# Loading 32 partitions of one expert's weights as four 8-partition DMAs, each followed by a tiny read

## The chip, the cores and the metric

The kernel runs on one core of one Trainium2 chip. The metric is device time in microseconds (us) of one execution. Most executions of one kernel agree within 0.3 to 0.5%. A time is "faster" or "slower" only when the 95% interval of the ratio leaves the band of 2% around one.

## The reference

The program is an attention layer followed by a soft mixture of experts. Cut to what matters:

```python
# q, k, v: (8 batches, 8 heads, 576, 64), fp32
scores = scale * q @ k^T          # heads 0-3: window of 32; heads 4-7: window of 128, every 4th
attn   = softmax(scores) @ v
x      = attn, heads side by side # (4608, 512)

logits = x @ phi                  # (4608, 32): 8 experts x 4 slots
slot_input = softmax(logits, over rows)^T @ x          # (32, 512)
for e in range(8):                                     # w1[e]: (512, 1024), w2[e]: (1024, 512), fp32
    slot_out[e] = relu(slot_input[e] @ w1[e]) @ w2[e]
out = softmax(logits, over slots) @ slot_out           # (4608, 512)
```

What matters for this change: the weights `w1` and `w2` are 2 MB per expert each and are read once, the output can't begin before the last expert's `w2` has landed, and nothing can be loaded usefully after that.

## The kernel before

All DMAs are issued by POOL on one queue. They convert fp32 in HBM to fp16 in SBUF while they copy. The weights of the experts are requested far ahead, between the attention batches. The loads of `w2`:

```python
def load_w2(e, half=None):
    if half is None:                       # one DMA: all 128 partitions, 1024 KB written
        nc.gpsimd.dma_start(
            out=w2t[e].rearrange("p (h l) n -> p h (l n)", h=2),
            in_=moe_w2[e].rearrange("(h p l) n -> p h (l n)", h=2, l=4),
        )
        return
    src = moe_w2[e].rearrange("(h p l) n -> h p l n", h=2, l=4)
    c0 = NH * half
    for h in range(2):                     # two DMAs: half of the columns, 256 KB written each
        nc.gpsimd.dma_start(
            out=w2t[e][:, 4 * h : 4 * h + 4, c0 : c0 + NH], in_=src[h][:, :, c0 : c0 + NH]
        )
```

The order in which they are requested; `weights(b, g)` is called twice in each batch b:

```python
HALVED = (6, 7)
ORDER = (0, 1, 4, 2, 3, 5) + HALVED

def weights(b, g):
    if b < B - 2:
        load_w1(*next_w1.pop(0))
    elif b == B - 2:
        if g == 0:
            ...                            # what is left of w1
            load_w2(0)
            load_w2(1)
        else:
            slab_weights(4, "vs0", V_SLAB) # expert 4 takes over a buffer of attention
            load_w2(4)
    elif g == 0:
        ...
        for e in (2, 3):
            w2t[e] = pool.tile([128, 8, DMODEL], FP16, name=f"w2_{e}", tag=f"w2_{e}")
            load_w2(e)
    else:
        slab_weights(5, "vs1", V_SLAB)
        load_w2(5)
        slab_weights(6, "qk0", QK_SLAB)
        slab_weights(7, "v0", V_SLAB)
        for half in range(2):
            for e in HALVED:
                load_w2(e, half)           # eight halved DMAs, the last loads of the program
```

The matmuls of `slot_out` use `w2` in `ORDER`, first for the left half of the output's columns, then for the right half. When the left halves of experts 6 and 7 have landed, the left half of the output is written while the right halves still load:

```python
slot_out(0, ORDER[:6])
slot_out(1, ORDER[:6])
slot_out(0, HALVED)
at = {5: 0}
for pair in range(NSPLIT // 2):
    combine(0, pair)                       # output rows, left columns: matmul, scale, DMA out
    if pair in at:
        slot_out(1, (HALVED[at[pair]],))
slot_out(1, HALVED[1:])
for pair in range(NSPLIT // 2, NFIN // 2):
    combine_full(pair)                     # further rows, all columns
```

The softmax here doesn't subtract the row's maximum and nothing guards it: scores larger than these inputs give would overflow.

Of the kernel before, what the change touches and what calls it, by code (L numbers as in the profile page):

```python
# [10 lines left out]
FP16 = mybir.dt.float16  # L11
# [38 lines left out]
def kernel(  # L50
# [10 lines left out]
    nc = tc.nc  # L61

    consts = ctx.enter_context(tc.tile_pool(name="consts", bufs=1))
    masks = consts.tile([128, W1 + NLEFT], FP16, name="masks")
    halves = consts.tile([128, 1], FP32, name="halves")
    bias = (
        masks[:, None, 0:WQ].broadcast_to([128, 3, WQ]),
        masks[:, 0 : W1 + NLEFT],
# [18 lines left out]
    w2t = {e: w2a_pool.tile([128, 8, DMODEL], FP16, name=f"w2_{e}", tag=f"w2_{e}") for e in range(2)}  # L87
# [12 lines left out]
    for i in range(NV):  # L100
        slab = fix.tile([128, V_SLAB], FP16, name=f"v{i}", tag=f"v{i}")
        n = NT * 4 * VW
# [5 lines left out]
    def slab_weights(e, tag, n):  # L108
        t = fix.tile([128, n], FP16, name=f"w2_{e}", tag=tag)
        w2t[e] = t[:, 0 : 8 * DMODEL].rearrange("p (c n) -> p c n", c=8)  # L110
# [99 lines left out]
    def load_w1(e, i):  # L210
        nc.gpsimd.dma_start(  # L211
            out=w1t[e][:, 2 * i : 2 * i + 2, :].rearrange("p l f -> p (l f)"),
            in_=moe_w1[e, 256 * i : 256 * i + 256].rearrange("(p l) f -> p (l f)", l=2),
        )

    def load_w2(e, half=None):
        if half is None:
            nc.gpsimd.dma_start(
                out=w2t[e].rearrange("p (h l) n -> p h (l n)", h=2),
                in_=moe_w2[e].rearrange("(h p l) n -> p h (l n)", h=2, l=4),  # L220
            )
            return
        src = moe_w2[e].rearrange("(h p l) n -> h p l n", h=2, l=4)
        c0 = NH * half
        for h in range(2):
            nc.gpsimd.dma_start(  # L226
                out=w2t[e][:, 4 * h : 4 * h + 4, c0 : c0 + NH], in_=src[h][:, :, c0 : c0 + NH]
            )
# [8 lines left out]
    def qk_dil(ti, b, part):  # L237
        src = raw[(ti, b)][:, 1, :].bitcast(U32)
        t = (qTd if ti == 0 else kTd)[b % 2]
        dst = t.rearrange("p s t -> p (s t)").bitcast(U32)  # L240
        base, n, step, j0 = ((0, 5, 292, 0), (2 * SUB, 4, -283, 2))[part]
        o = bass.AP(dst.tensor, dst.offset + base, [dst.ap[0], (SUB, 2), (1, n), (9, 16), (step, 2)])
        i = bass.AP(src.tensor, src.offset + 32 * j0, [src.ap[0], (32, 2), (128, n), (1, 32)])
        nc.vector.transpose(out=o, in_=i)  # L244
# [217 lines left out]
    def prologue():  # L462
# [56 lines left out]
            qk_dil(0, 0, part)  # L519
        qk_dil(1, 0, 0)  # L520

    HALVED = (6, 7)
    ORDER = (0, 1, 4, 2, 3, 5) + HALVED
    late_pools = []
# [6 lines that stand above are left out]
                while next_w1:  # L531
# [4 lines that stand above are left out]
                slab_weights(4, "vs0", V_SLAB)  # L536
                load_w2(4)
        elif g == 0:
            raw_pool.release()
            pool = tc.alloc_tile_pool(name="w2b", bufs=1, side="right")  # L540
            late_pools.append(pool)
            for e in (2, 3):
                w2t[e] = pool.tile([128, 8, DMODEL], FP16, name=f"w2_{e}", tag=f"w2_{e}")
                load_w2(e)
        else:
            slab_weights(5, "vs1", V_SLAB)
            load_w2(5)
            slab_weights(6, "qk0", QK_SLAB)
            slab_weights(7, "v0", V_SLAB)
            for half in range(2):  # L550
                for e in HALVED:
                    load_w2(e, half)

    def slot0(b):
        att, b1, b2, b3 = b < B, b - 1 >= 0 and b <= B, 2 <= b < B + 2, b + 1 < B
        if att:
            qk_dil(1, b, 1)
            emit_scores(b, 0)
            if b + 2 < B:
                load_qk(0, b + 2)  # L560
                load_qk(1, b + 2)
            weights(b, 0)
# [29 lines left out]
    def slot1(b):  # L592
        att, b1, b3 = b < B, 1 <= b <= B, b + 1 < B
        if b3:
            qk_plain(0, b + 1)
        if att:
            emit_scores(b, 1)
            if b == 0:
                order_v_plain(b)
            spread_v(b)  # L600
            if b + 2 < B:
                load_v(b + 2)
            weights(b, 1)
            emit_av(b, "p", 0)
            emit_norm(b, "p", 0)
        if b1:
            back_xT_dil(b - 1, 0)
        if b3:
            qk_plain(1, b + 1)
        if b1:  # L610
            back_xT_dil(b - 1, 1)
# [41 lines left out]
    for g in range(4):  # L653
# [8 lines left out]
        out=diag,  # L662
# [7 lines left out]
    for fc in range(2):  # L670
        for g in range(2):
            for dc in range(4):
                for j in range(4):
                    e = 4 * g + j
# [32 lines left out]
    def slot_out(half, experts):  # L707
        for e in experts:
            for c in range(8):
                g, j, a = e // 4, e % 4, c % 4  # L710
                nc.tensor.matmul(
                    so[half][32 * a : 32 * a + 32, :],
                    hTm[2 * g + c // 4][:, c % 4, 32 * j : 32 * j + 32],
                    w2t[e][:, c, NH * half : NH * half + NH],
                    start=(e == ORDER[0] and c < 4),
                    stop=(e == ORDER[-1] and c >= 4),
                )
        if experts[-1] == ORDER[-1]:
            nc.scalar.copy(out=so_sb[:, NH * half : NH * half + NH], in_=so[half])
# [75 lines left out]
    with tc.manual_schedule(engines=None):  # L795
# [5 lines that stand above are left out]
            combine(0, pair)  # L801
# [4 lines that stand above are left out]
# [39 lines left out]
```

## Time and profile before

| | before |
|---|---|
| median of three runs (lowest to highest) | 183.85 us (183.4 to 183.96) |
| span in the profile, mean granted clock of TensorE | 182.0 us, 0.902 |
| last landing of expert 5's `w2` | 145.26 us |
| last `w2` DMA: first engine lands, last engine lands | 152.23 us, 155.98 us |
| last landing of an output DMA | 179.27 us |

The landing times in the last three rows come from the completion events in the trace: it holds sixteen of them for every DMA (1,472 for 92 DMAs), which I take for one report from each of the sixteen DMA engines. "Last landing" is the sixteenth report; the "spread" of a DMA is the time from its first report to its last.

These lines are from the page of the kernel before. In the first two each entry is one of 40 equal slices of the span: the busy tenths of the sixteen DMA engines, and what they moved. Then come two DMA queues (packets, megabytes, share of the engines' time) and the shares of the chain of work that ended last.

```profile
DMA  4999999999999999999999999999999999999992
GB/s 61 194 195 210 202 211 212 204 212 214 201 213 214 201 212 216 200 212 212 205 210 215 202 215 213 214 213 214 216 214 216 195 196 181 355 404 404 409 409 59
...
q0 software_dynamic: 29248, 40.41, 117.6%
q8 instruction: 19, 0.31, 0.6%
...
DMA 40%; PE 37%; ACT 6%; DVE 5%; POOL 4%; issue 3%; POOLq 0%
```

The DMA engines are busy in nearly every slice, at about 195 to 216 GB/s while fp32 is read and fp16 is written, and at about 404 to 409 GB/s while results are written. So the kernel is bound by the DMA engines from the first load to the last store.

This is POOL's timeline of the kernel before: start, duration, engine, line and operation, output and input, count; in brackets, how long POOL had been idle just before and what ended the wait. L218 is a whole `w2` DMA, here the one of expert 5, and L226 a halved one.

```profile
116.29 0.72 POOL L218 DMA_DIRECT2D w<-in_moe_w_dram  x1
117.00 1.49 POOL L226 DMA_DIRECT2D w<-in_moe_w_dram  x2
120.25 0.74 POOL L226 DMA_DIRECT2D w<-in_moe_w_dram  x1 [1.76 <-ACT p L292]
124.95 0.74 POOL L226 DMA_DIRECT2D w<-in_moe_w_dram  x1 [3.96 <-DMA w<-in_moe_w_dram]
129.92 0.74 POOL L226 DMA_DIRECT2D w<-in_moe_w_dram  x1 [4.22 <-DMA w<-in_moe_w_dram]
...
145.54 0.74 POOL L226 DMA_DIRECT2D w<-in_moe_w_dram  x1 [4.21 <-DMA w<-in_moe_w_dram]
```

Expert 5 and the first halved DMA are requested at 116 to 117 us and land at 145.3 and 146.6 us, so the queue holds almost 30 us of work. The waits from 124.95 us on show how deep it may get. Each issue waits for the landing of the DMA issued eight before it: the issue at 124.95 comes 0.28 us after the landing, at 124.67, of the DMA issued at 102.18. The trace agrees: the completions are counted on eight semaphores in turn. I call these the eight places. There is always something in the queue, which the windows of the kernel before show near the end of the loads (start and end, width, busy time and count of PE, PE's weight loads, DVE, ACT and POOL, then granted clock, DMA share, GB/s; the share can exceed one, as that of q0 does on the page):

```profile
146.00:148.00 2.00, 1.21 (x48) 1.01 (x37) 0.00 (x0) 0.00 (x0) 0.28 (x1) 1.00 1.45 195
148.00:150.00 2.00, 0.50 (x8) 0.12 (x8) 0.00 (x0) 0.00 (x0) 0.00 (x0) 0.93 1.45 196
150.00:152.00 2.00, 0.88 (x7) 0.56 (x7) 0.00 (x0) 0.44 (x2) 0.00 (x0) 0.50 1.45 196
```

The DMA rate doesn't move from 195 GB/s, while PE idles between halved DMAs. The sixteen engines don't keep step. These are the sixteen completion times of two DMAs of the kernel before, sorted, counted from the first:

```
expert 5, landing 141.54 to 145.26:  0.0 0.1 0.3 0.4 0.5 0.5 1.1 1.2 2.1 2.2 2.2 2.2 2.7 2.8 3.2 3.7
last w2,  landing 152.23 to 155.98:  0.0 0.1 0.3 0.5 0.5 0.5 1.1 1.2 2.1 2.2 2.2 2.7 2.8 3.3 3.3 3.8
```

Eight engines are 0 to 1.2 us behind the first, the other eight 2.1 to 3.8 us. The kernel's end hangs on the slowest one. That is the imbalance which the change wants to use.

### The profile page before, as it was taken

Reading aid. Unit: us, or ns where it says so; the run is one execution under the profiler, and the core shown is the slowest. Engines: PE = TensorE matmul, PEld = TensorE weight load, DVE = VectorE, ACT = ScalarE, POOL = GpSimd, SP = SyncE. Lnnn points to the kernel's source line nnn. Section 1 sums busy time; section 2 is a strip of 40 time slices with the busy share of each in tenths; the row PEclk is TensorE's granted clock in tenths of the full one; section 3 lists DMA queues with packets and bytes.
Section 4 is the critical chain, followed back from the end, with each engine's and each line's share of the span. In section 5 each row is a group of like instructions: output and inputs, shape, how many; then the busy total and the mean of one; then the engine's idle time right before and its main releaser. Section 6 shows DMA issues by size and latency. Waiting matters only on the chain.

```text
span 182.0 us, 5571 instructions
## 1 busy us (share of the span) xinstructions
PE 143.0 (79%) x2464; PEld 85.3 (47%) x2464; DVE 107.1 (59%) x232; ACT 90.4 (50%) x162; POOL 80.8 (44%) x118
## 2 busy tenths in 40 slices
PE   0467987999999999999999999999879447885000
PEld 0234545656646746746746746746443334331000
DVE  4688785865884984984984984445041104597000
ACT  2044355847557657657657657655101105696000
POOL 7954563634624434432631625621111014999700
PEclk9999998798799999999999999999756995799755
DMA  4999999999999999999999999999999999999992
GB/s 61 194 195 210 202 211 212 204 212 214 201 213 214 201 212 216 200 212 212 205 210 215 202 215 213 214 213 214 216 214 216 195 196 181 355 404 404 409 409 59
DMA packets 29271, 40.75 MB, mean 224 GB/s; under 512 B 1600, under 2 KB 19008, under 8 KB 29248
## 3 DMA queue, kind: packets, MB, share of 16 engines
q0 software_dynamic: 29248, 40.41, 117.6%
q8 instruction: 19, 0.31, 0.6%
q14 instruction: 4, 0.03, 0.0%
HBM read 61.93 MB, written 9.44 MB: 392 GB/s over the span
## 4 chain that ended last, share of the span: by engine, by line
DMA 40%; PE 37%; ACT 6%; DVE 5%; POOL 4%; issue 3%; POOLq 0%
DMA w<-in_moe_w_dram 26%; DMA raw<-in_k_dram 10%; PE lg L407 6%; PE o_p L338 5%; PE sa L281 4%; ACT p L292 4%; PE sa L270 4%; DMA out_dram<-ot 3%; PE sb L270 3%; PE f L745 2%; PE vb L162 2%; PE va L162 2%; PE rd L388 2%; PE u L451 2%; POOL out_dram L791 1%
## 5 line engine op out<-in xcount | busy, mean ns | idle before, releaser
L292 ACT ACTIVATE p<-sa 128x960 f16<-128x960 f32 (+2 forms) x24 | 21.4, 891 | 31.2 <-PE sb L281 30.6
L338 PEld LDWEIGHTS <-p 128*128 128x128 f16 (+2 forms) x544 | 19.8, 99 | 12.8 <-issue 8.6
L244 DVE STREAM_TRANSPOSE qk<-raw 128x320 uint32<-128x320 uint32 (+1 forms) x32 | 21.6, 679 | 0.3
L292 ACT ACTIVATE p<-sb 128x960 f16<-128x960 f32 (+2 forms) x24 | 21.2, 884 | 0.0
L235 DVE STREAM_TRANSPOSE qk<-raw 128x576 uint32<-128x576 uint32 x16 | 19.8, 1249 | 1.5 <-DMA raw<-in_k_dram 1.1
L211 POOL DMA_DIRECT2D w<-in_moe_w_dram x16 | 8.8, 553 | 26.3 <-DMA vs<-in_v_dram 12.7
L270 PE MATMUL sa<-masks,ident 128*128 128x480 f16 (+2 forms) x48 | 14.6, 390 | 7.3 <-POOL masks L488 6.2
L407 PE MATMUL lg<-xTd,phi 128*128 128x288 f16 x32 | 18.2, 657 | 0.0
L270 PEld LDWEIGHTS <-ident 128*128 128x128 f16 x96 | 9.1, 106 | 17.9 <-issue 7.0
L281 PEld LDWEIGHTS <-qk 32*128 32x128 f16 x832 | 12.3, 98 | 11.1 <-issue 8.9
L338 PE MATMUL o_p<-v,p 128*128 128x65 f16 (+1 forms) x288 | 16.8, 203 | 0.8 <-ACT v L171 0.7
L281 PE MATMUL sa<-qk 32*128 32x160 f16 (+4 forms) x416 | 16.2, 215 | 0.8 <-DVE qk L235 0.7
L226 POOL DMA_DIRECT2D w<-in_moe_w_dram x8 | 5.9, 744 | 23.3 <-DMA w<-in_moe_w_dram 21.6
L281 PE MATMUL sb<-qk 32*128 32x160 f16 (+4 forms) x416 | 16.3, 215 | 0.0
L360 DVE TENSOR_TENSOR xp<-o_p,rc_p 128x448 f16<-128x448 f32 (+1 forms) x24 | 14.4, 602 | 0.8
L360 DVE TENSOR_TENSOR xd<-o_d,rc_d 128x448 f16<-128x448 f32 (+1 forms) x24 | 14.4, 602 | 0.8
L270 PE MATMUL sb<-masks,ident 128*128 128x480 f16 (+2 forms) x48 | 14.4, 386 | 0.2 <-ACT p L292 0.2
L208 POOL COPY v<-v 32x1024 f16<-32x1024 f16 x8 | 8.3, 1036 | 11.3 <-DVE v L201 9.9
L162 PE MATMUL va<-vs,orders 32*128 32x256 f16 (+1 forms) x96 | 12.1, 289 | 1.0 <-ACT p L292 1.0
L411 ACT ACTIVATE ET<-lg 128x288 f16<-128x288 f32 x16 | 6.6, 411 | 11.8 <-PE lg L407 11.7
L381 ACT COPY xTp<-rp 128x576 f16<-128x576 f16 x16 | 10.4, 647 | 1.8 <-PE rp L376 1.8
L767 POOL DMA_DIRECT2D out_dram<-ot x15 | 10.8, 719 | 0.0
(102 smaller groups left out, 266.4 us busy)
## 6 DMA issues: line engine op xcount, KB each, us to landing
w<-in_moe_w_dram POOLq DMA_DIRECT2D x16, 512.0 KB, 17.0
w<-in_moe_w_dram POOLq DMA_DIRECT2D x6, 1024.0 KB, 25.3
out_dram<-of POOLq DMA_DIRECT2D x10, 512.0 KB, 6.2
vs<-in_v_dram POOLq DMA_DIRECT2D x8, 512.0 KB, 17.0
raw<-in_q_dram POOLq DMA_DIRECT2D x7, 576.0 KB, 18.2
raw<-in_k_dram POOLq DMA_DIRECT2D x7, 576.0 KB, 18.5
out_dram<-ot POOLq DMA_DIRECT2D x15, 256.0 KB, 4.9
w<-in_moe_w_dram POOLq DMA_DIRECT2D x8, 256.0 KB, 23.8
```

Of the source, the lines that this page charges most:

```text
L162: nc.tensor.matmul(o.rearrange("p (h d) -> p h d", h=4), l, st[:, 0:4, D * r : D * r + D], start=(r == 0), stop=(r == DIL - 1), skip_group ...
L211: nc.gpsimd.dma_start(out=w1t[e][:, 2 * i : 2 * i + 2, :].rearrange("p l f -> p (l f)"), in_=moe_w1[e, 256 * i : 256 * i + 256].rearrange( ...
L235: nc.vector.transpose(out=dst, in_=src)
L244: nc.vector.transpose(out=o, in_=i)
L270: nc.tensor.matmul(sps[h // 2][:, h % 2, 0:n], ident, bias[g], start=True, stop=False, skip_group_check=True,)
L281: nc.tensor.matmul(sps[h // 2][:, h % 2, c0 : c0 + w], kt_[32 * h : 32 * h + 32, k0 : k0 + 128, tt], qt_[32 * h : 32 * h + 32, q0 : q0 + w ...
L292: nc.scalar.activation(out=pt, in_=sps[ab][:, :, 0:n], func=AF.Exp, scale=SCALE)
L338: nc.tensor.matmul(o[p0 : p0 + np_, n, :], l, rr, start=(k == 0), stop=(k == len(jobs) - 1), skip_group_check=True,)
L360: nc.vector.tensor_tensor(out=x.rearrange("p t (h d) -> p (t h) d", h=4)[0:nq, u0:u1, :], in0=o[0:nq, 0:n, 0:D], in1=rc[0:nq, 0:n, None].b ...
L381: nc.scalar.copy(out=xTp_t[b][:, c, :], in_=rg)
L407: nc.tensor.matmul(lp, phi4[:, kc].rearrange("p c s -> p (c s)"), rhs, start=(kc == 0), stop=(kc == 3))
L767: nc.gpsimd.dma_start(out=out[r0 : r0 + 256, NH * half : NH * half + NH].rearrange("(k p) n -> p k n", k=2), in_=ot,)
```

## The change

The intent: an 8-partition DMA should be carried by eight of the sixteen DMA engines only. The last 32 partitions of expert 2 are taken out of its large DMA and requested as four DMAs over 8 partitions each (rows 96+j, 100+j, ...). After each of them stands a tiny read of 8 rows of 32 bytes, which should use the other eight engines, so that the next 8-partition DMA returns to the first eight. The data of 32 partitions would then lie on the eight engines that have time left, and the slow eight would have less to carry. The whole diff:

```diff
@@ constants
+    turn = consts.tile([128, 8], FP16, name="turn")
@@ load_w2
-    def load_w2(e, half=None):
+    def load_w2(e, half=None, rows=slice(0, 128)):
         if half is None:
             nc.gpsimd.dma_start(
-                out=w2t[e].rearrange("p (h l) n -> p h (l n)", h=2),
-                in_=moe_w2[e].rearrange("(h p l) n -> p h (l n)", h=2, l=4),
+                out=w2t[e].rearrange("p (h l) n -> p h (l n)", h=2)[rows],
+                in_=moe_w2[e].rearrange("(h p l) n -> p h (l n)", h=2, l=4)[rows],
             )
             return
@@ before weights
+    def load_w2_eight(e, j):
+        load_w2(e, rows=slice(96 + j, 128, 4))
+        nc.gpsimd.dma_start(out=turn[0:8, :], in_=moe_w2[e, 0:8, 0:8])
+
@@ weights, last batch
                 w2t[e] = pool.tile([128, 8, DMODEL], FP16, name=f"w2_{e}", tag=f"w2_{e}")
-                load_w2(e)
+                load_w2(e, rows=slice(0, 96 if e == 2 else 128))
         else:
             slab_weights(5, "vs1", V_SLAB)
+            load_w2_eight(2, 0)
             load_w2(5)
+            for j in range(1, 4):
+                load_w2_eight(2, j)
             slab_weights(6, "qk0", QK_SLAB)
```

Below, d0 to d3 are the four 8-partition DMAs of data and r0 to r3 the four tiny reads. All four reads write the same 8 by 8 elements of `turn`, which nothing uses.

## The prediction

> **What bounds the kernel now.** The page's DMA row is 9 in nearly every slice (200-216 GB/s while fp32 is read and fp16 written, 404-409 GB/s while results are written): DMA-bound from about 5 to 179 us. The sixteen completion events of each DMA in the trace show that engines do not keep step: the last w2 transfer lands between 152.2 us (first engine) and 156.0 us (last). Eight engines lag 0-1.2 us, eight 2.2-3.8 us. Eighteen instruction packets of 16 KB (0.9 us each, durations repeating with period eight) run between 18 and 140 us, and the lags grow in steps of about 1.1 us, so eight engines seem to carry all instruction fetches. (Trainium skill, "Runtime: NRT & Kernel Launch", Instruction fetch mechanics: 16 KiB blocks on the sequencer's own queue; the trace agrees: queue 8, 16,384 B.) The slowest engine is never idle: last weights 155.98 + 9.44 MB of output at 405 GB/s (23.3 us) = 179.3 us; the last landing is 179.27.
>
> **Intent and gain.** The Trainium skill ("DMA: Bandwidth & Descriptors", How many engines) says an 8-partition DMA goes to 8 consecutive engines from a cursor; no trace here shows it yet. The tiny read on the other eight returns the cursor, so all 32 partitions land on the same eight engines: 10 partitions of expert 2 there, 6 on the others. A 128-partition w2 DMA (8 per engine) takes 4.9 us, so a partition is 0.61 us: -1.22 us on one half, +1.22 us on the other. If the fetching half is relieved, the best case is -1.2 us (182.6).
>
> **Cost.** POOL's timeline shows each DMA waiting for the landing of the one eight issues earlier (issue at 124.95 waits for that of 102.18, landed 124.67). Eight small DMAs now fill these places. And all four tiny reads write the same tile, so I expect each to wait until the previous one has landed (write after write). Read 0 lands behind w2(3), near 139.1 us (140.3 - 1.2). Read 1 then goes behind w2(5), landing near 144.1. Read 2 goes into an almost empty queue, landing near 145.9 (0.5 us issue, 0.7 to first packet, 0.6 to land, estimated from the first DMA and the output DMA at 152.7). Read 3 goes then, and the first halved w2 DMA only at about 146.4, first packet 147.6; in before these eight were queued from 117 us on. They take 10.7 us (145.26 to 155.98): end near 158.9 instead of 156.0. Half 0 is complete near 153.5 instead of 150.6, and the outputs shift as much, all on the critical path: +2.9 us. If the strided row slices (97,101.. against 96,100..) also count as overlapping, another +0.9 us. PE, ACT, DVE have slack.
>
> **Prediction.** 186.9 us, 80% range 183.5 to 188.4. Faster by over 2%: 0.02; within: 0.65; slower: 0.33.
>
> **What would show it.** POOL's timeline: read 1 waiting to about 139, read 2 to about 144, eight halved w2 issues back to back (0.74 us) from 146-147 us. DMA row: a hole near 144-147.5 us. Completion spread of the last w2 DMA about 1 us instead of 3.8; of w2(5) nearer 2.5 than 3.7 if the fetching half was relieved, about 5 if loaded. PE: the so matmuls (L711) wait for w2 to 153-154 us. Output DMAs as in before, shifted.
>
> **What would make it wrong.** If the reads do not wait for each other, only the eight places bind: halves from about 139.7 us, no hole, 182.5-185, the sign set by which half the cursor picks. If rows overlap, 187.7. If small DMAs land later than 1.7 us in an emptying queue, more.

## The result, and the profile after

| | before | after |
|---|---|---|
| median of four runs (lowest to highest) | 183.91 us (183.4 to 184.42) | 191.68 us (190.96 to 192.04) |
| span in the profile, granted clock | 182.0 us, 0.902 | 190.0 us, 0.874 |
| first halved DMA issued | 117.00 | 147.94 |
| expert 5's `w2`, last landing | 145.26 | 144.47 |
| last `w2` DMA, first and last landing | 152.23, 155.98 | 161.10, 163.35 |
| last landing of an output DMA | 179.27 | 186.65 |

The kernel after is slower: the ratio is 1.0418, with a 95% interval of 1.0376 to 1.046. A ratio is the mean time of one kernel's fast runs over the mean of the other's fast runs of the same rounds, so it isn't quite the ratio of the medians quoted. The time lies above the predicted range of 183.5 to 188.4 us.

The page of the kernel after, the same lines as above:

```profile
DMA  4999999999999999999999999999991699999990
GB/s 67 195 202 205 211 211 215 201 210 212 208 208 212 208 213 204 209 213 207 208 212 205 213 214 215 214 214 216 211 185 20 91 177 212 375 358 405 412 405 8
...
q0 software_dynamic: 29504, 40.41, 113.1%
q8 instruction: 19, 0.31, 0.6%
...
PE 45%; DMA 24%; ACT 8%; POOL 7%; DVE 6%; issue 4%; POOLq 0%
...
L525 POOL DMA_DIRECT2D turn<-in_moe_w_dram x4 | 2.1, 530 | 24.8 <-DMA turn<-in_moe_w_dram 24.8
```

The same 40.41 MB are moved, in 256 more packets. The thirty-first slice (142.5 to 147.25 us) holds a hole: 20 GB/s where the kernel before has 216 in its thirty-first slice. The group line of the four reads says why: POOL was busy for 2.1 us with them and stood for 24.8 us in front of them, waiting for a DMA into `turn`.

POOL's timeline of the kernel after, with the columns as before. L219 is a whole or 8-partition DMA of `w2`, L525 a tiny read, L227 a halved DMA.

```profile
116.00 0.58 POOL L219 DMA_DIRECT2D w<-in_moe_w_dram  x1
116.58 0.54 POOL L525 DMA_DIRECT2D turn<-in_moe_w_dram  x1
117.10 0.75 POOL L219 DMA_DIRECT2D w<-in_moe_w_dram  x1
119.81 0.57 POOL L219 DMA_DIRECT2D w<-in_moe_w_dram  x1 [1.95 <-DMA w<-in_moe_w_dram]
139.90 0.53 POOL L525 DMA_DIRECT2D turn<-in_moe_w_dram  x1 [19.52 <-DMA turn<-in_moe_w_dram]
140.41 0.58 POOL L219 DMA_DIRECT2D w<-in_moe_w_dram  x1
145.25 0.53 POOL L525 DMA_DIRECT2D turn<-in_moe_w_dram  x1 [4.26 <-DMA turn<-in_moe_w_dram]
145.77 0.59 POOL L219 DMA_DIRECT2D w<-in_moe_w_dram  x1
147.42 0.53 POOL L525 DMA_DIRECT2D turn<-in_moe_w_dram  x1 [1.06 <-DMA turn<-in_moe_w_dram]
147.94 5.93 POOL L227 DMA_DIRECT2D w<-in_moe_w_dram  x8
```

From top to bottom: d0, r0, expert 5, d1, r1, d2, r2, d3, r3, and the eight halved DMAs. r1 waits 19.5 us until r0 has landed (139.61 us, behind expert 3 in the queue), r2 until r1 has landed (144.97, behind expert 5), and r3 until r2 has landed (146.87). While r1 waits, nothing behind it is issued. The queue drains, expert 5 lands at 144.47 us, and the halved DMAs, which were queued since 117 us in the kernel before, go out only from 147.94 us. The windows of the kernel after:

```profile
144.00:146.00 2.00, 0.00 (x0) 0.00 (x0) 0.00 (x0) 0.00 (x0) 0.75 (x2) 0.91 0.04 6
146.00:148.00 2.00, 0.00 (x0) 0.00 (x0) 0.00 (x0) 0.00 (x0) 0.94 (x3) 0.50 0.21 29
148.00:150.00 2.00, 1.16 (x24) 1.04 (x28) 0.00 (x0) 0.00 (x0) 2.00 (x3) 0.50 0.26 28
150.00:152.00 2.00, 2.00 (x45) 1.72 (x41) 0.00 (x0) 0.00 (x0) 2.00 (x4) 0.50 1.25 165
152.00:154.00 2.00, 0.85 (x23) 0.61 (x13) 0.00 (x0) 0.00 (x0) 1.86 (x3) 0.88 1.31 163
154.00:156.00 2.00, 0.45 (x8) 0.21 (x8) 0.00 (x0) 0.00 (x0) 0.00 (x0) 0.97 1.39 183
156.00:158.00 2.00, 0.65 (x8) 0.21 (x4) 0.00 (x0) 0.37 (x1) 0.00 (x0) 0.50 1.46 197
```

For six us, next to nothing moves. Then the rate is 163 to 165 GB/s for four us, 183 for two more, and reaches the 195 to 197 GB/s of the kernel before only after 156 us. The granted clock is 0.5 in some of these windows, but PE isn't what the time hangs on: after 152.8 us it waits again for halved DMAs, as in the kernel before. Next is the chain that ended last in the kernel before, in order of time (start, duration, what it was):

```profile
102.18 22.49 DMA w<-in_moe_w_dram
124.67 0.28 issue
124.95 25.66 DMA w<-in_moe_w_dram
```

And the same of the kernel after:

```profile
116.58 23.03 DMA turn<-in_moe_w_dram
139.90 5.07 DMA turn<-in_moe_w_dram
145.25 1.61 DMA turn<-in_moe_w_dram
...
153.12 10.23 DMA w<-in_moe_w_dram
```

The chain before is two weight DMAs linked by a freed place. After, it is three tiny reads, one behind the other, and then the last halved DMA. Notice that the share of DMA in this chain fell, from 40% to 24%, and yet the DMA engines still decide the end. A share of the chain doesn't say which resource has no slack.

From the last landing of `w2` on, everything is only shifted. The outputs end 23.29 us after it before and 23.30 us after it after. So the 7.37 us by which the last `w2` comes later (155.98 to 163.35) is the whole shift of the last output (7.38 us). The span grew by 8.0 us and the median by 7.8; the remaining 0.6 us of the span lies behind the last output's landing and wasn't looked into.

### The profile page after: what moved, and what is told of

Its sections match the earlier page's. It is cut to its first block, busy times and chain, and to the rows that moved or that the text cites. A ratio compares the mean times of both kernels' runs of the same rounds, so it can differ in the third digit from the quotient of the medians.

```text
span 190.0 us, 5584 instructions
## 1 busy us (share of the span) xinstructions
PE 144.8 (76%) x2464; PEld 86.9 (46%) x2464; DVE 107.2 (56%) x232; ACT 90.4 (48%) x162; POOL 85.0 (45%) x126
## 3 DMA queue, kind: packets, MB, share of 16 engines
q0 software_dynamic: 29504, 40.41, 113.1%
## 4 chain that ended last, share of the span: by engine, by line
PE 45%; DMA 24%; ACT 8%; POOL 7%; DVE 6%; issue 4%; POOLq 0%
DMA turn<-in_moe_w_dram 16%; PE lg L408 8%; ACT p L293 7%; PE o_p L339 7%; PE sa L282 6%; DMA w<-in_moe_w_dram 5%; PE sa L271 5%; PE sb L271 4%; DMA out_dram<-ot 3%; PE u L452 3%; PE vb L163 3%; PE va L163 3%; PE rd L389 2%; POOL w L227 2%; DVE of L792 2%
## 5 line engine op out<-in xcount | busy, mean ns | idle before, releaser
L212 POOL DMA_DIRECT2D w<-in_moe_w_dram x16 | 8.8, 553 | 26.9 <-DMA vs<-in_v_dram 12.5
L719 PE MATMUL so<-w,hTm 128*32 128x256 f16 x128 | 7.4, 371 | 11.2 <-DMA turn<-in_moe_w_dram 6.0
L361 DVE TENSOR_TENSOR xd<-o_d,rc_d 128x448 f16<-128x448 f32 (+1 forms) x24 | 14.5, 602 | 0.8
L361 DVE TENSOR_TENSOR xp<-o_p,rc_p 128x448 f16<-128x448 f32 (+1 forms) x24 | 14.5, 602 | 0.8
L525 POOL DMA_DIRECT2D turn<-in_moe_w_dram x4 | 2.1, 530 | 24.8 <-DMA turn<-in_moe_w_dram 24.8
```

Source lines behind the costliest of these rows:

```text
L212: nc.gpsimd.dma_start(out=w1t[e][:, 2 * i : 2 * i + 2, :].rearrange("p l f -> p (l f)"), in_=moe_w1[e, 256 * i : 256 * i + 256].rearrange( ...
L361: nc.vector.tensor_tensor(out=x.rearrange("p t (h d) -> p (t h) d", h=4)[0:nq, u0:u1, :], in0=o[0:nq, 0:n, 0:D], in1=rc[0:nq, 0:n, None].b ...
```

## The experiments

Three theories to begin with. A: the cost is the chain of reads through one tile (each read waits for the one before), and with it the empty queue. B: the cost is the eight places, which eight small DMAs take up. C: the 8-partition DMAs of data are slow themselves, or load the wrong eight engines. The diffs are cut to the lines that matter. The first four kernels ran on one chip, beside eleven runs of the kernel before with a median of 183.87 us.

### own_columns: the reads get columns of their own

```diff
-    turn = consts.tile([128, 8], FP16, name="turn")
+    turn = consts.tile([128, 32], FP16, name="turn")
-        nc.gpsimd.dma_start(out=turn[0:8, :], in_=moe_w2[e, 0:8, 0:8])
+        nc.gpsimd.dma_start(out=turn[0:8, 8 * j : 8 * j + 8], in_=moe_w2[e, 0:8, 0:8])
```

> The changed kernel, but each tiny read writes its own eight columns of the turn tile, so no read has to wait for another; same number, order and size of DMAs. Chain theory (the loss is the reads waiting for each other): the first halved w2 DMA is issued near 140 us instead of 147.9, no hole in the DMA row, time 183 to 185 us. Rival 1 (eight more DMAs in eight places are the loss): the second halved DMA waits for w2 expert 5 (near 144.5 us) and the time stays above 188 us. Rival 2 (uneven engines are the loss): time stays above 188 us and the last w2 DMA has a spread over 5 us.

Measured: 186.89 us, ratio 1.0178 (1.015 to 1.0207). The chain of waits between the reads is gone, and that gives back 4.8 of the 7.8 us. But the time is still 3 us above the kernel before (by the 2% rule this is "unclear", as the interval reaches over 1.02), which is outside of what I expected. POOL's timeline of own_columns shows the rest:

```profile
139.48 0.53 POOL L525 DMA_DIRECT2D turn<-in_moe_w_dram  x1
140.00 0.80 POOL L227 DMA_DIRECT2D w<-in_moe_w_dram  x1
144.65 5.13 POOL L227 DMA_DIRECT2D w<-in_moe_w_dram  x7 [3.86 <-DMA w<-in_moe_w_dram]
```

The second halved DMA waits until 144.65 us, for expert 5, which landed at 144.37. It was issued eight before, and all the places between are taken by d1 to d3, r1 to r3 and one halved DMA. When it goes, little but one halved DMA is in the queue. This is theory B at work, and the windows of own_columns show its smaller hole, 60 GB/s and then 134 to 147 where the kernel before has 195:

```profile
144.00:146.00 2.00, 1.33 (x44) 1.07 (x48) 0.00 (x0) 0.33 (x1) 1.35 (x2) 1.00 0.44 60
146.00:148.00 2.00, 1.63 (x60) 1.43 (x53) 0.00 (x0) 0.00 (x0) 2.00 (x4) 1.00 1.16 147
148.00:150.00 2.00, 0.29 (x4) 0.10 (x4) 0.00 (x0) 0.00 (x0) 1.79 (x3) 1.00 1.14 141
```

So A and B aren't exclusive: with the chain removed, the places bind and cost about 3 us.

### other_half: the read stands before its data

Own columns as above, and the two lines of `load_w2_eight` exchanged. If a tiny read passes the turn to the other eight engines, this puts the data on the other eight.

> As own_columns, but each tiny read goes before its data DMA, so that the cursor, if there is one, puts the data on the other eight engines. Cursor-and-skew theory: this run and own_columns differ by up to 2.4 us, the spread of the last w2 DMA being about 2.5 us where the data went to the eight engines without instruction fetches and 5 to 6 us where it went to the fetching ones. If the cursor does not matter, or each half has as many fetching engines, the two agree within 0.5 us.

Measured: 186.95 us, ratio 1.0173 (1.0147 to 1.0199), 0.06 us from own_columns. So exchanging read and data makes no difference in time here. That it puts the data on the other half isn't shown; the pairs further down speak against it.

### no_reads: the four data DMAs without the reads

```diff
         load_w2(e, rows=slice(96 + j, 128, 4))
-        nc.gpsimd.dma_start(out=turn[0:8, :], in_=moe_w2[e, 0:8, 0:8])
```

> The four data DMAs over 8 partitions without the tiny reads; with a cursor the data alternates between the halves and both carry 8 partitions. Chain theory: no chain, only four more DMAs than before: within 0.5 us of before (183.5 to 184.5). Rival (small DMAs themselves are dear): over 186 us.

Measured: 184.24 us, ratio 1.002 (0.9996 to 1.0043). Against theory C: to request 32 partitions as four DMAs costs 0.4 us, by the interval at most 0.8. With four small DMAs instead of eight, halved DMAs are queued from 129.94 us on.

### reads_alone: the four reads without the split data

```diff
     def load_w2_eight(e, j):
-        load_w2(e, rows=slice(96 + j, 128, 4))
         nc.gpsimd.dma_start(out=turn[0:8, :], in_=moe_w2[e, 0:8, 0:8])
@@ expert 2 is loaded whole
-                load_w2(e, rows=slice(0, 96 if e == 2 else 128))
+                load_w2(e, rows=slice(0, 128))
```

> Expert 2 is loaded whole as before; the four tiny reads into one tile stand where the change has them. Chain theory: the reads alone bring nearly the whole loss: first halved w2 DMA issued near 148 us, hole in the DMA row from about 145 to 149 us, time 190.5 to 192.5 us. Rival 2 (uneven engines): within 1 us of before.

Measured: 191.31 us, ratio 1.0433 (1.0394 to 1.0472). Four reads of 256 bytes, which carry nothing, bring the whole loss. They add only four DMAs, as no_reads does, so theory B isn't needed for it. With own_columns, where the chain goes and 4.8 us come back, this shows that A is the cause. The halved DMAs are issued from 148.43 us on, and the last `w2` lands at 162.96.

### What the pairs do to the sixteen engines

The intended gain never came, in any kernel. In the next two kernels the four pairs move to a quiet place: expert 0 instead of expert 2, one pair in each of batches 2 to 5, so that no wait and no hole can hide an effect. In spread_pairs each read stands behind its data, in spread_turned before it.

```diff
             load_w1(*next_w1.pop(0))
+            if g == 0 and 2 <= b < 6:
+                load_w2_eight(0, b - 2)
@@ expert 0
-                load_w2(0)
+                load_w2(0, rows=slice(0, 96))
```

> The four data-and-read pairs taken off expert 2 and given to expert 0, whose tile is free from the start: one pair in each of four batches of the attention stage, each read into its own columns. Same bytes, same 32 partitions on eight engines, but at most two small DMAs in the eight places at a time and none near the end. If the data lands on the eight engines without instruction fetches, as own_columns suggests (the seven or eight engines that lag least finish its small data DMA about 0.5 us after the DMA before, most others 0.2 us), the last w2 DMA spreads 2.5 us instead of 3.8 and the time is 182.5 to 183.2 us, 0.7 to 1.2 under before. If it lands on the fetching ones: spread 5 us, 185 us. If placement does not matter: within 0.3 us of before.

> As spread_pairs with the read ahead of its data DMA. If a cursor chooses the eight engines, this goes the other way from spread_pairs (about 185 us, spread about 5 us, or the reverse). If the engines follow from the partitions written, both agree within 0.4 us.

Measured: 184.41 us (ratio 1.0027, 1.0008 to 1.0046) and 184.21 us (1.0007, 0.9987 to 1.0026), beside 183.96 us. The completion times of the last `w2` spread over 3.5 and 4.0 us, against 3.8 in the kernel before. A concentration of 32 partitions on eight engines should have moved this by about 1.2 us one way in one kernel and the other way in the other. It did neither (spread_pairs is 0.45 us above the kernel before by the medians, a little more than the 0.3 us forecast for "placement does not matter"); this is a miss of the intended mechanism itself.

pairs_8 doubles the dose: eight pairs, over experts 0 and 1, one at every turn of batches 2 to 5. pairs_512 makes each read larger, 512 columns of 8 rows, in case 32 bytes a row are too few to count (the reads use three column blocks in rotation).

```diff
+            if 2 <= b < 6:
+                load_w2_eight(g, b - 2)
...
-        nc.gpsimd.dma_start(out=turn[0:8, :], in_=moe_w2[e, 0:8, 0:8])
+        c = 8 * (4 * e + j)                                                         # pairs_8
+        nc.gpsimd.dma_start(out=turn[0:8, c : c + 8], in_=moe_w2[e, 0:8, 0:8])
or
+        c = 512 * ((2 * j + e) % 3)                                                 # pairs_512
+        nc.gpsimd.dma_start(out=turn[0:8, c : c + 512], in_=moe_w2[e, 0:8, 0:512])
```

> As spread_pairs, but for experts 0 and 1: eight data-and-read pairs, one in each slot of four batches. If the tiny read brought the choice of engines back, eight engines would now carry 64 partitions alone, 4.9 us of work more than the other eight: the spread of the last w2 DMA would be 2.5 to 3 us in the opposite sense or over 6 us, and the time at least 1 us away from before. If the tiny read does not turn it, data alternates, every engine carries the same, the spread stays 3.4 to 4.2 us and the time within 1 us of before.

> As pairs_8, but each read takes 512 columns (2048 B a row, 1024 B written) in place of 8 columns (32 B). If only a larger read turns the choice of engines, the spread of the last w2 DMA becomes over 6 us (187 us or more) or the sense of the lag turns over. If reads of neither size turn it, this agrees with pairs_8 within 0.7 us.

Measured: 184.99 us (1.0043, 1.0 to 1.0086) and 184.62 us (1.0036, 1.0002 to 1.007), beside 183.93 us. The completion times of pairs_8, sorted and counted from the first, cut to a few of the sixteen:

```
before the pair:          0.0 0.1 0.1 0.1 0.3 0.4 0.7 0.8 ... 2.5
after one data DMA:       0.0 0.5 0.6 0.7 0.8 1.0 1.1     ... 3.0
after the next data DMA:  0.0 0.0 0.1 0.3 0.5 0.7 0.7 0.9 ... 2.5
```

One 8-partition DMA moves a part of the engines out of line, and the next one brings them back. The first of the sixteen reports shows it eight times over: from the DMA before it to the data DMA it moves by 0.28, 0.63, 0.26, 0.63, 0.22, 0.64, 0.17 and 0.63 us, and 0.61 us is the work of one partition. So consecutive data DMAs go to different halves and level each other out, although a read stands between them. (pairs_8 lies just outside of what was forecast for this: 1.06 us above the kernel before and a spread of 4.31 us, where within 1 us and 3.4 to 4.2 were expected; pairs_512 has 3.25.)

The last pair of kernels asks this more directly and has no reads at all. Each group of 8 partitions is loaded as two DMAs of unequal size, columns 0 to 1535 and 1536 to 2047. If same-shaped DMAs alternate between two halves of the engines, the large ones all fall on one half, and exchanging the two moves them to the other.

```diff
     def load_w2_eight(e, j):
-        load_w2(e, rows=slice(96 + j, 128, 4))
-        nc.gpsimd.dma_start(out=turn[0:8, :], in_=moe_w2[e, 0:8, 0:8])
+        for cols in (slice(0, 1536), slice(1536, 2048)):     # exchanged in unequal_small_first
+            load_w2(e, rows=slice(96 + j, 128, 4), cols=cols)
```

> As pairs_8, but instead of data and a wasted read, each group of 8 partitions comes as two useful DMAs of the same form, first three quarters of the columns, then one quarter. pairs_8 and pairs_512 showed the lags going out of line after one data DMA and back after the next, so consecutive data DMAs go to different halves whatever the read between. If the halves alternate for DMAs of one form, eight engines now get 48 partitions' worth and the other eight 16, 2.45 us of work apart: spread of the last w2 DMA about 2 to 2.7 us and a time of 182.5 to 183.3 us if the lagging half is relieved, over 5.5 us and 185 us if it is loaded. If the choice is not by alternation: spread 3.2 to 4.3 us and within 1 us of before.

> As unequal_big_first with the quarter ahead of the three quarters. If the halves alternate, this is the mirror image: where that one gains, this one loses by about as much, 2 us or more apart. If not, the two agree within 0.5 us.

Measured: 184.81 us (1.0057, 1.0036 to 1.0079) and 186.28 us (1.0138, 1.0115 to 1.0161), beside 183.87 us. The order of the two is worth 1.47 us in time, and 1.35 us in the last landing of `w2` (156.12 and 157.47 us). That lies between the two forecasts (2 us or more apart, or within 0.5), and neither kernel got faster. It fits the alternation that pairs_8 shows: load can be placed on one half by size. But even in the better order the slowest engines aren't relieved. The sorted times of its last `w2` are these:

```
0.0 0.3 2.0 2.1 2.2 2.2 2.3 2.3 2.5 2.6 2.9 3.0 3.1 3.3 4.2 4.3
```

Six engines that had slack were filled, two were not, and the two worst are at 4.2 and 4.3 us, where the worst of the kernel before is at 3.8. My reading is that the eight engines of a half aren't the eight that lag, so that no order of halves can help them; this is argued from these lines, not shown. Why the tiny read doesn't take part in the alternation stays open. None of these versions beats the kernel before.

### What an empty queue costs

The prediction knew the chain of reads and the hole, and still was 4.8 us too low (it gave 0.65 to a time within 2% of the kernel before and 0.33 to a slower one). What was open: after the hole the eight halved DMAs took longer than I had allowed. whole_after loads experts 6 and 7 of the kernel after as two large DMAs instead of eight halved ones, whole_before does it to the kernel before. If small DMAs or strided 512-byte runs make the restart slow, it should vanish.

```diff
-            for half in range(2):
-                for e in HALVED:
-                    load_w2(e, half)
+            for e in HALVED:
+                load_w2(e)
```

> The changed kernel, with experts 6 and 7 loaded whole (256 packets of 4096 B each) instead of in four halves each (512 packets of 512 B). The chain of reads and the hole stay: first of the two issued at about 148 us. If the slow restart comes from the halved DMAs being issued into an empty queue, the last w2 landing comes 10.5 to 11.3 us after the first packet (9.8 us of transfer and a landing), near 160 to 160.7 us, instead of 13.95 us after it (163.35). If any transfer restarts slowly: over 12.5 us. Time itself is not the point, since the first half of the output can no longer start early.

> Control for whole_after: the kernel before with experts 6 and 7 loaded whole. Queue never empties: the last w2 landing near 155 to 156 us, about 9.8 us after that of expert 5.

Measured, one look each (state unknown): 194.32 and 187.92 us. With no halves, the output's left half can't be written early, so only the loads are compared. In whole_before experts 6 and 7 take 9.7 us from expert 5's landing to the last landing of `w2` (145.34 to 155.07). In whole_after they take 11.3 us from the first packet (149.87) to the last landing (161.16), against 13.9 us in the kernel after (149.43 to 163.35). That is the upper edge of the forecast for "the halved DMAs restart slowly" (10.5 to 11.3), and not the one for "any transfer does" (over 12.5). Still, a part of the slow start is there with large DMAs too. Count from the issue, with 1.2 us to the first packet and 0.6 us to land as in the prediction: 11.5 us allowed (1.2 + 9.7 + 0.6), 12.9 taken (148.30 to 161.16), so 1.3 us too many. For the kernel after the same sum gives 2.9 us too many, of which an instruction packet (see below) makes 1.05. The first seven packets of whole_after took 793 to 944 ns where a packet of this size takes 324 ns in the stream, the rate is 213 GB/s from 151.5 us on, and the second large DMA lands 4.85 us after the first, as in the stream. So by this one look some 1.3 us belong to the empty queue with DMAs of either size, and the rest, some 0.5 us, may belong to the halves.

The last three kernels give the dose. They are reads_alone with two, three and six reads, and nothing else:

```diff
             load_w2(5)
-            for j in range(1, 4):
+            for j in range(1, 2):        # reads_2; range(1, 3) in reads_3, range(1, 6) in reads_6
                 load_w2_eight(2, j)
```

> reads_alone with two tiny reads instead of four. The second read waits for the first (about 141 us), but the halved DMAs follow it at once, behind expert 5's data, which lands near 145.5 us: no hole. If only an empty queue costs: 183.5 to 184.8 us. If the waiting reads cost in themselves: 187 us or more.

> Three reads: the third waits for the second, which lands with expert 5 near 145.8 us, so the first halved DMA is issued near 146.6 us, 1.85 us earlier than with four reads. Fixed restart cost and 1.85 us a read: 189.0 to 190.0 us, that is 5 to 6 us over before although the queue is empty only about 2.5 us. If the restart cost grows with the length of the hole: 187 us or less.

> Six reads: two more round trips of 1.87 us each in an empty queue (issue to issue, 146.08 to 147.95 in reads_alone). Fixed restart cost: 191.31 + 3.74 = 194.6 to 195.5 us. If the restart gets dearer with the hole: over 196 us.

| | reads_2 | reads_3 | reads_alone (4) | reads_6 |
|---|---|---|---|---|
| median, us | 184.45 | 189.66 | 191.31 | 195.30 |
| ratio (95%) | 1.0028 (1.0007 to 1.005) | 1.0311 (1.0282 to 1.034) | 1.0433 (1.0394 to 1.0472) | 1.0619 (1.0591 to 1.0647) |
| kernel before in the same rounds | 183.83 | 183.83 | 183.87 | 183.83 |
| first halved DMA issued | 140.89 | 146.32 | 148.43 | 152.10 |
| expert 5, last landing | 144.78 | 145.15 | 145.64 | 145.54 |
| last `w2`, last landing | 156.14 | 161.27 | 162.96 | 167.32 |
| first halved issue to last landing | 15.25 | 14.95 | 14.53 | 15.22 |

reads_2 is the control: its second read waits for 22 us, as in the others, but the halved DMAs are still issued 3.9 us before expert 5 has landed. POOL's timeline of reads_2:

```profile
140.36 0.54 POOL L524 DMA_DIRECT2D turn<-in_moe_w_dram  x1 [22.11 <-DMA turn<-in_moe_w_dram]
140.89 5.92 POOL L227 DMA_DIRECT2D w<-in_moe_w_dram  x8
```

It loses 0.6 us (by the interval at most 0.9). A wait of 22 us in front of the queue is nearly free, as long as the queue isn't empty at its end. One read more and the queue runs dry: plus 5.2 us from reads_2 to reads_3, though the halved DMAs are issued only 1.2 us after expert 5's landing. From there each read adds 1.65 us (to four reads) and 2.0 us (to six), which is about one round trip of a tiny read. POOL's timeline of reads_6 shows the trips directly, 1.84 to 1.92 us from issue to issue:

```profile
147.84 0.50 POOL L524 DMA_DIRECT2D turn<-in_moe_w_dram  x1 [1.33 <-DMA turn<-in_moe_w_dram]
149.68 0.50 POOL L524 DMA_DIRECT2D turn<-in_moe_w_dram  x1 [1.34 <-DMA turn<-in_moe_w_dram]
151.60 0.51 POOL L524 DMA_DIRECT2D turn<-in_moe_w_dram  x1 [1.42 <-DMA turn<-in_moe_w_dram]
152.10 5.93 POOL L227 DMA_DIRECT2D w<-in_moe_w_dram  x8
```

After a hole, the way from the first halved issue to the last landing is 14.5 to 15.2 us in these three kernels and 15.4 in the kernel after, whether the hole was short or long. (In reads_2 the 15.25 us include 3.9 us behind expert 5.) In these runs the cost of the restart doesn't grow with the length of the hole. It can be laid out DMA by DMA: time from the first halved issue to its last landing, then from each last landing to the next.

```
                 first   second to eighth                      sum
in the stream            1.29 1.34 1.39 1.32 1.30 1.34 1.42          (kernel before)
after             3.77   2.72 1.38 1.31 1.32 1.34 2.39 1.19    15.42
reads_3           3.68   2.46 1.76 1.30 1.34 1.40 2.03 0.98    14.95
reads_alone       3.56   2.39 1.57 1.63 1.33 1.34 1.46 1.25    14.53
reads_6           3.71   2.52 1.70 1.31 1.33 1.37 2.09 1.19    15.22
```

In all four the first DMA needs 3.6 to 3.8 us, the second comes 2.4 to 2.7 us later, and by the fourth or fifth the pace of 1.3 us is there. The first steps alone are slow. The step of 2.4 us at the seventh DMA of the kernel after is another thing: an instruction packet of 16,384 bytes at 159.7 us set one engine back, and the spread of the completion times grew from 1.36 to 2.41 us. (The others have such a packet too, at 158.03 us in reads_3, 159.46 in reads_alone and 163.78 in reads_6. In reads_3 and reads_6 the step at the seventh DMA is 2.0 to 2.1 us; in reads_alone it is 1.46, and the spread shrinks there from 1.31 to 1.05 us, so that packet seems to have met an engine that had time left.)

The slow rate alone isn't the mark of an empty queue. In reads_2 the queue never ran dry, yet its windows dip as well:

```profile
144.00:146.00 2.00, 1.48 (x56) 1.29 (x52) 0.00 (x0) 0.00 (x0) 2.00 (x3) 1.00 1.19 151
146.00:148.00 2.00, 0.91 (x28) 0.55 (x21) 0.00 (x0) 0.00 (x0) 0.81 (x2) 1.00 1.41 180
148.00:150.00 2.00, 0.32 (x8) 0.10 (x4) 0.00 (x0) 0.00 (x0) 0.00 (x0) 1.00 1.37 181
```

There the halved DMAs still land every 1.33 to 1.54 us up to the sixth, while the spread shrinks from 2.06 to 1.23 us: the engines that were ahead lost time, and the slowest didn't. What reads_2 doesn't have is the late first and second landing.

In all fifteen kernels that keep the halved loads, the last output lands 23.26 to 23.33 us after the last `w2`. Nothing of what the experiments changed acts on any other path.

## Why the prediction was wrong

What held:

- **DMA-bound, and the path to the end.** In the kernel after "the slowest engine is never idle" isn't true of the hole, but the sum "last weights + 23.3 us" held to 0.04 us in fifteen kernels.
- **The four reads wait for each other, write after write.** r1 was issued at 139.90, r2 at 145.25, r3 at 147.42, then eight halved issues back to back, and the DMA row has its hole from about 144 us. own_columns takes these waits away by changing the columns alone.
- **Row slices don't count as overlapping.** d1 went out at 119.81 while d0 was still in flight (it landed at 139.44), and d2 at 140.41 while d1 was (144.81). When d3 went out, all three had landed.
- **PE, ACT and DVE have slack.** They only follow.

What failed is one term, and a smaller one beside it:

- **"They take 10.7 us (145.26 to 155.98): end near 158.9."** The 10.7 us were read from a queue that was never empty. From the first halved issue (146.4) to the end (158.9) the prediction allowed 12.5 us: 1.2 to the first packet, eight steps of 1.34, and 0.6 to land. The runs show 15.4 us. By the steps above, and compared with that allowance, the first DMA took 0.6 us more (3.77 against 3.14), the second 1.4 us more, the instruction packet at the seventh cost 1.05, and the other five were 0.15 us faster: 2.9 us in sum. The slow start comes with the empty queue: reads_3, reads_alone and reads_6 have it without the split data, and reads_2, with the same long wait but no empty queue, doesn't. How much of it comes with halved DMAs only is open: whole_after has 1.3 us of it, and the kernel after 1.9 without the instruction packet.
- **"The first halved w2 DMA only at about 146.4."** It was 147.94, 1.5 us later. Of this, r0 landed 0.5 us later than predicted (139.61 for 139.1), r1 0.4 us more (144.97 for 144.1), r2's own trip was 0.1 us longer, and POOL took 0.55 us from r2's landing to r3's issue where I had counted none.
- 1.5 and 2.9 us make 4.4, and so the last `w2` came at 163.35 instead of 158.9: plus 7.4 us, where plus 2.9 was predicted. The time follows, 191.7 for 186.9.
- **"If the reads do not wait for each other, only the eight places bind [...] no hole, 182.5-185."** own_columns has a small hole and takes 186.9. I had counted the places only up to the first halved DMA (about 139.7 predicted, 140.00 measured), not to the second, which waits for expert 5 until 144.65.
- **"All 32 partitions land on the same eight engines."** No run shows that; in pairs_8, which asks it of eight pairs, the data DMAs alternate, with a read between each two. The expected relief of 1.2 us, or its opposite, appears nowhere: the spread of expert 5's completion times went from 3.72 to 3.97 us, neither to 2.5 nor to 5, and that of the last `w2` is 2.25, where about 1 was predicted.

The part of the change that reads the machine rightly is that an 8-partition DMA uses eight engines. In the kernel after, d3 falls into the empty queue, and its sixteen reports show it: eight come within 0.1 us of the first, and eight 1.2 to 1.5 us later.

```
d3: 0.0 0.0 0.0 0.1 0.1 0.1 0.1 0.1 1.2 1.2 1.3 1.3 1.3 1.3 1.5 1.5
r2: 0.0 0.0 0.0 0.0 0.0 0.1 0.1 0.1 0.1 0.1 0.1 0.1 0.2 0.2 0.2 0.2
```

The Trainium skill says so ("DMA: Bandwidth & Descriptors", How many engines, in the section on why a DMA increments its semaphore by 16): a DMA on POOL's path goes to the largest number k up to 16 that divides the slowest dimension of both its access patterns, and for k under 16 to k consecutive engines from a round-robin cursor. The trace agrees as far as k = 8 for d3, and pairs_8 and the unequal pairs agree with a cursor that moves. By the same rule the reads over 8 rows should move it as well; no run here shows that they do, and pairs_8 speaks against it. Yet the data of a read is split in eight too: the packets of r2 and of r3 are eight of 16 bytes each, up to six of them in flight at once, and 24 of 4 bytes.

What stays open: why the first two DMAs after an empty queue land late, how much of that belongs to the halved DMAs, why the rate dips for some 6 us (28, 165, 163, 183, 197 GB/s in the kernel after, but 151, 180, 181 in reads_2 too), and why the tiny reads don't take part in the alternation.

## What to carry to other kernels

A transfer that carries almost nothing can still cost several us, if its destination makes it wait for an earlier one and everything behind it stands in the same queue; give such dummies destinations of their own, and count the places in the queue that they take. Ask of every wait in front of a DMA queue whether the queue is empty when it ends: a wait of 22 us in front of a full queue cost 0.6 us, and one read more, which let it run dry, cost 5.2. When you estimate what comes after a hole, don't use durations read from a full stream: here eight DMAs that take 10.7 us in the stream needed 14.5 to 15.4 from their first issue.

## What the Trainium skill lacked or had wrong

- No page that I looked up gives the cost of a DMA queue that has run empty beyond the fixed cost of one DMA. Here the first 256 KB DMA after a hole landed 3.6 to 3.8 us after its issue and the second 2.4 to 2.7 us after the first, against 1.34 us in the stream. It would belong to "DMA: Bandwidth & Descriptors", Anatomy of one DMA.
- The same section gives a fixed cost of about 2.0 us per DMA. A tiny read in an empty queue took 1.6 us here from issue to its last landing (145.25 to 146.87 and 147.42 to 149.01), and 1.84 to 1.92 us from issue to issue in a chain of such reads.
- The rule for the number and choice of engines (same page, How many engines) doesn't say what a tiny read does to the cursor. In spread_pairs, spread_turned, pairs_8 and pairs_512 a read of 8 rows between 8-partition DMAs changed neither the time (ratios 1.0007 to 1.0043) nor the spread (3.25 to 4.3 us, 3.8 before) as a turn of eight engines would have, while the order of two unequal data DMAs was worth 1.47 us.
- "Runtime: NRT & Kernel Launch", Instruction fetch mechanics, calls the cost of crossing a 16 KiB boundary "mostly hidden", and doesn't speak of the DMAs that share an engine with the fetch. Here the packet of 16,384 bytes at 159.7 us set one DMA engine of the kernel after back by about 1.1 us (the spread went from 1.36 to 2.41 us), and in a DMA-bound kernel the slowest engine decides the end. It isn't so for every packet: that of reads_alone at 159.46 us didn't widen the spread.
